# A spectral mixer on one core: sixteen f32 transforms become triples of F32R products with split constants, and the last one moves to the head of its row

## Chip, core and metric

The kernel runs on one core of a Trainium2 chip. Five engines matter: TensorE (PE in the profile, with its weight loads listed apart as PEld), VectorE (DVE), ScalarE (ACT), GpSimd (POOL) and SyncE (SP), which only starts transfers. The metric is device time in microseconds (us), the median of repeated runs. The views of the profile show one profiled execution, with its own time.

## What is computed

```python
x = A_x                                    # (1, 2048, 512)
xn = _layernorm(x)
X = rfft2(xn) * (w_r + 1j * w_i)
s = irfft2(X)                              # spectral branch
h = _layernorm(xn)                         # token-mixing branch
u = gelu(einsum("bsd,sf->bdf", h, w1) + b1)        # f = 1792
y = einsum("bdf,fs->bds", u, w2) + b2
out = x + s * silu(y.transpose(0, 2, 1))
```

Both branches start from the normalised rows of x. All inputs and outputs are float32.

## The kernel before

The 2048 tokens are laid out as 128 partitions by NJ = 16 rows; row j is a tile of 128 x 512. F32R is a 32-bit type that TensorE multiplies in one pass, with fewer bits than f32. A product that is to keep f32's accuracy is therefore made of three: with a = ah + al and b = bh + bl, where the high part is a rounding to F32R and the low part is what the rounding left, it is ah·bh + ah·bl + al·bh. The profile prints TensorE's operands as f32 for either type; on ACT and DVE the outputs of a split are printed fp32r.

**First stage (lines 388 to 521).** A loop over the rows j does three things on TensorE:

- `hidden_early(j, 4, 0, w[0], ...)`: w1's columns for four blocks of 128 hidden units times h(j), into PSUM banks 0 to 3. Four products with w1's high part and h's high part `hh[j]`, four with w1's low part and `hh[j]`, four with w1's high part and h's low part `hl[j]`. All are 128x128 weights against 512 moving columns, in F32R, on line 395.
- between the second and the third four, `first_transform(h, c)` (line 223): four f32 products that turn h(j)'s 512 channels by the constant `c`, into bank 7. The weights are h's blocks of 128 columns and the 128 columns of `c` are moving. `c` is the transform matrix `cf` times a number per token, `m["q"]`, which takes back the second normalisation; `turned` (line 217) makes it by one ACT instruction per row.
- `hidden_early(j, 3, 4, w[1], ...)`: nine more F32R products, for banks 4 to 6.

While TensorE works on row j, the other engines prepare row j + 1: ACT normalises it to `h` (line 209), rounds it to `hh` and w1's two pieces to `w1h` (line 387); DVE subtracts for the low parts `hl` and `w1l` (line 390). ACT copies bank 7 to `zt` (line 231, `first_copy`). `fold` (lines 234 to 250) combines zt's quarters into `ey`, the input of the second stage: DVE makes `o`, `e` and `t` (lines 236 to 240), POOL adds and subtracts e's halves (lines 242 and 243), ACT moves half of `o` across partitions once `t` is done (line 244), and DVE writes the last two groups of `ey` (line 247). The fold of row j is issued during row j + 1, piece by piece, because `fold` is a generator.

What fixes the order: instructions wrapped in `keep` stay on their engine in the order in which they are written; others are placed by a scheduler before the program runs. Pools hand out buffers: a tile with `bufs=1` is rewritten only after every reader of its former content is done.

**From the first stage to the second.** Row 14's turn issues three transfers `w1s` on POOL's queue (`w1_raw`, line 447), the raw w1 of the first three parts of the second batch of hidden units. After the loop `gelu(2, 2)` and `gelu(1, 1)` empty banks 2 and 1 on ACT (line 290) into `u`, `w1_high` rounds `w1s` to `w1h` on ACT, `w1_low` makes `w1l` on DVE, and `run(folds)` finishes row 15's fold.

**Second stage (lines 525 to 751).** The order of everything is written out in the string `STEPS`, one letter per piece of a stream. TensorE takes the products of the second batch (lines 678, 679, 681 and 687) in turn with the spectral filter: `along_channels` (line 586, f32, reads `ey` and `cd`, writes banks 4 to 7 in the order 7, 6, 5, 4), `forward` (line 600) and `way_back` (line 665). Before a bank can be written, the gelu that empties it must be done: bank 6, 5 and 4 by `gelu(9, 6)`, `gelu(8, 5)` and `gelu(7, 4)`.

**Third stage.** The products with w2 (line 941, F32R, 256 moving columns, three for each pair) and the inverse transforms.

Of the kernel before, what the change touches and what calls it, by code (L numbers as in the profile page):

```python
# [8 lines left out]
F32 = mybir.dt.float32  # L9
F32R = mybir.dt.float32r  # L10
BF16 = mybir.dt.bfloat16
AF = mybir.ActivationFunctionType
ALU = mybir.AluOpType
PSUM = bass.MemoryType.PSUM

P = 128
S, D, F = 2048, 512, 1792
NJ = 16
# [100 lines left out]
def spectral_mixer_kernel(tc, x, w1, b1, w2, b2, wk, we, wx, c_f, c_ft, c_d, c_i, c_g, c_h, c_s, out):  # L119
    nc = tc.nc  # L120
    V, A, G, T, SY = nc.vector, nc.scalar, nc.gpsimd, nc.tensor, nc.sync
    keep = tc.keep_in_program_order
# [8 lines left out]
    def pool(stack, side, name, bufs):  # L131
        return stack.enter_context(tc.tile_pool(name=name, bufs=bufs, side=side, reuse_waits="tile"))
# [9 lines left out]
    with tc.tile_pool(name="ps", bufs=1, space=PSUM) as psp, ExitStack() as left, ExitStack() as right:  # L142
        ps = psp.tile([P, 8, 512], F32, name="ps")
        pers = pool(left, "left", "pers", 1)
        cf = pers.tile([P, P], F32, name="cf")
# [20 lines left out]
        lnp = pool(rstage, "right", "ln", 2)  # L166
        wbp = pool(rstage, "right", "w1b", 3)
        hs = [new_hu(f"h{j}") for j in range(NJ)]
        hh, hl = [h[:, 0] for h in hs], [h[:, 1] for h in hs]
# [6 lines left out]
        def moments(nm, n):  # L176

            return {k: lnp.tile([P, 2, w], F32, name=f"{k}{nm}", tag="m" + k, bufs=3)[:, :n]  # L180
                    for k, w in (("st", 6), ("mv", 2), ("v2", 2), ("sd", 2), ("r0", 2), ("t", 2), ("rs", 2), ("nb", 1),
                                 ("q", 1))}
# [31 lines left out]
        def new_h(j):  # L214
            return lnp.tile([P, D], F32, name=f"h{j}", tag="h")

        def turned(j, m, i):

            c = lnp.tile([P, P], F32, name=f"cf{j}", tag="cfj")
            keep(A.activation(c, cf, AF.Copy, scale=m["q"][:, i]))  # L220
            return c

        def first_transform(h, c):
            z = ps[:, 7].rearrange("p (b c) -> p b c", c=P)
            for b in range(4):
                T.matmul(z[:, b], h[:, b * P:(b + 1) * P], c, start=True, stop=True)  # L226
            return z

        def first_copy(j, z):
# [37 lines left out]
        def run(steps):  # L267
            for _ in steps:
                pass
# [11 lines left out]
        def ordered(instruction):  # L281
            return keep(instruction) if strict else instruction
# [3 lines left out]
        def gelu(ft, bank):  # L286
            i, half = ft % NH, ft // NH
            if i not in raw:
                raw[i] = usp.tile([P, 2, D], F32, name=f"u{i}", tag="u")
            ordered(A.activation(raw[i][:, half], ps[:, bank], AF.Gelu_apprx_tanh, bias=b1t[:, ft:ft + 1]))  # L290
# [101 lines left out]
        def hidden_early(j, nf, bank, w, between):  # L392
            def products(wi, hj, first, last):
                for i in range(nf):
                    T.matmul(ps[:, bank + i], w[wi][:, i * P:(i + 1) * P], hj, start=first and j == 0, stop=last and j == NJ - 1)  # L395
            products(0, hh[j], True, False)
            products(1, hh[j], False, False)
            r = between()
            products(0, hl[j], False, True)
            return r  # L400

        m = moments("m0", 2)
        for i, c_ in enumerate(halves):
# [2 lines left out]
        m = {k: t[:, :1] for k, t in m.items()}  # L406
        roots(m)
        w = w1_tiles(0, *WA), w1_tiles(0, *WB)
        h = new_h(0)
# [9 lines left out]
        c = turned(0, m, 0)  # L419
# [4 lines left out]
        m = moments("m2", 2)  # L424
# [3 lines left out]
        raws_, parts, mids = {}, {}, []  # L428
# [14 lines left out]
        def w1_raw(i):  # L443
            place_, bufs = (mids[0], 1) if i % 4 == 3 else (w1p, 3)
            raws_[i] = place_.tile([P, 4 * P], F32, name=f"w1s{i}", tag="w1r", bufs=bufs)[:, :part_width(i)]
            for to, cols in w1_runs(i, raws_[i]):
                (SY if mids else G).dma_start(to, cols)

        def w1_high(i):
            parts[i] = [w1p.tile([P, 4 * P], F32R, name=f"w1{c}_{i}", tag="w1" + c)[:, :part_width(i)] for c in "hl"]  # L450
            A.activation(parts[i][0], raws_[i], AF.Copy)

        def w1_low(i):
            V.tensor_sub(parts[i][1], raws_[i], parts[i][0].bitcast(F32))
# [1 line left out]
        folds = iter(())  # L456
        for j in range(NJ):
            more = j + 1 < NJ
            if more:
                raws[j + 1, 0], raws[j + 1, 1] = w1_load(j + 1, *WA), w1_load(j + 1, *WB)  # L460
            if j == 0:
                load_x(3)
                load_x(4)
                SY.dma_start(b1t, b1)
                SY.dma_start(b2t, b2)
            if j == 4:
                SY.dma_start(cd, c_d)
                G.dma_start(cft, c_ft)
            if j in (6, 8, 10, 12):
                q = slice(16 * (j - 6), 16 * (j - 4))  # L470
                SY.dma_start(out[q, :NJ - 1], x[q, :NJ - 1])
            z = hidden_early(j, 4, 0, w[0], lambda: first_transform(h, c))
            hidden_early(j, 3, 4, w[1], lambda: None)

            early = j > 0
            if more:
                w = w1_tiles(j + 1, *WA), w1_tiles(j + 1, *WB)
                h = new_h(j + 1)
                normed(h, xs[j + 1], *of[j + 1])
                high(hh[j + 1], h)  # L480
                if early and j + 3 < NJ:
                    stats(of[j + 3][0], of[j + 3][1], xs[j + 3])
                    if j % 2 == 0:
                        spreads(of[j + 2][0], 2)
            for _ in range(3):
                next(folds, None)
            if more:
                high(w[0][0], raws[j + 1, 0])
            next(folds, None)
            if more:  # L490
                if early and j % 2 == 0 and j + 2 < NJ:
                    scales(of[j + 2][0])
                low(w[0][1], raws[j + 1, 0], w[0][0])
                if not early:
                    stats(m, 0, xs[2])
                high(w[1][0], raws[j + 1, 1])
                low(hl[j + 1], h, hh[j + 1])
                c = turned(j + 1, *of[j + 1])
                if not early:
                    stats(m, 1, xs[3])  # L500
                    spreads(m, 2)
            run(folds)
            if more:
                low(w[1][1], raws[j + 1, 1], w[1][0])
                if not early:
                    scales(m)
                if j % 2 == 0 and j + 4 < NJ:
                    m = moments(f"m{j + 4}", 2)
                    of.update({j + 4: (m, 0), j + 5: (m, 1)})
            if j + 5 < NJ:  # L510
                load_x(j + 5)
            folds = fold(j, first_copy(j, z))
            if j == NJ - 2:
                for i in range(3):
                    w1_raw(i)
        gelu(2, 2)
        w1_high(0)
        w1_low(0)
        gelu(1, 1)
        run(folds)  # L520
        w1_high(1)
        rstage.close()

# [2 lines left out]
        V, A, G, SY = map(in_order, free)  # L526
# [227 lines left out]
        V, A, G, SY = free  # L754
# [165 lines left out]
        for p in range(NP):  # L920
# [7 lines left out]
            for k, n in enumerate(ORDER):  # L928
                wf = ready.pop(0)
                w = next(wforms, None) if len(ready) < 2 else None  # L930
# [85 lines left out]
```

## Time and profile before

| what | value |
|---|---|
| median of 3 runs | 381.93 us (381.85 to 384.48) |
| the profiled execution | 382.29 us, span 380.5 us |
| TensorE busy over the span | 369.8 us, 97% |
| VectorE, ScalarE, GpSimd busy | 81%, 56%, 27% |
| granted TensorE clock | 1.00 |
| first stage, from its first product to the second stage's first | 6.33 to 98.13 us |

A span is what lies between the first and the last instruction of the program; the profiled execution's time is 1.8 us longer. "Busy" for TensorE counts a product until its modelled end, and neighbours overlap, so the spacing of starts says more about TensorE's rate than the duration of one product. A row of a timeline gives the start, the length, the engine, the line, the operation, output and inputs, the shape, the number of instructions merged into it, and in brackets the idle time before it with what ended that.

### The profile page before, as it was taken

The numbers are of one execution on the slowest core, as the hardware profiler recorded it, in microseconds if no ns is written. First come the engines' busy times: TensorE is split into PE (matmuls) and PEld (weight loads), VectorE is DVE, ScalarE is ACT, GpSimd is POOL, SyncE is SP. The second block draws the span as 40 slices with busy tenths as digits, with TensorE's granted clock in tenths as the row PEclk, the third lists the DMA queues.
The fourth block names the chain that finished last, engine by engine and source line by source line (L and its number), as shares of the span: only waits on it lengthen the run. The fifth ranks groups of instructions, "written<-read, shape, count | busy, mean of one in ns | idle before, by whom it ended". The sixth has DMA issues, their size and how long they took to land.

```text
span 380.5 us, 7482 instructions
## 1 busy us (share of the span) xinstructions
PE 369.8 (97%) x2760; PEld 327.8 (86%) x2760; DVE 309.0 (81%) x660; ACT 213.3 (56%) x384; POOL 102.3 (27%) x133
## 2 busy tenths in 40 slices
PE   8999999999999999999999799999999999999994
PEld 4888888888877676777779799999999999999994
DVE  5899999865799999999967798776767768777763
ACT  4677755754972365865456765545555555545541
POOL 2133233243511735765400011020303020200100
PEclk9999999999999999999999999999999999999999
DMA  7956467214455767999866599898888888895602
GB/s 249 323 190 231 133 222 239 91 42 128 120 196 179 253 213 258 283 280 307 194 181 155 149 267 188 265 164 263 168 246 184 223 204 193 194 217 158 100 0 56
DMA packets 41945, 73.32 MB, mean 193 GB/s; under 512 B 4180, under 2 KB 25172, under 8 KB 41780
## 3 DMA queue, kind: packets, MB, share of 16 engines
q1 hardware_dynamic: 35460, 58.88, 48.6%
q0 software_dynamic: 6448, 13.96, 21.4%
q8 instruction: 21, 0.34, 0.4%
q14 instruction: 16, 0.13, 0.1%
HBM read 60.24 MB, written 8.13 MB: 180 GB/s over the span
## 4 chain that ended last, share of the span: by engine, by line
PE 86%; DVE 8%; issue 2%; ACT 2%; DMA 1%; SPq 0%; DVEq 0%; ACTq 0%
PE ps L941 34%; PE ps L395 19%; PE ps L678 6%; PE ps L679 5%; PE ps L226 4%; PE ps L687 4%; PE ps L866 4%; PE ps L586 4%; PE ps L875 4%; DVE pq L128 2%; DVE e L128 2%; PE ps L665 1%; PE ps L681 1%; PE ps L600 1%; DMA x<-in_x_dram 1%
## 5 line engine op out<-in xcount | busy, mean ns | idle before, releaser
L395 PE MATMUL ps<-h,w1h 128*128 128x512 f32 x224 | 58.5, 398 | 0.0
L395 PEld LDWEIGHTS ps<-h,w1h 128*128 128x128 f32 x224 | 40.8, 188 | 8.1 <-ACT w1h L387 0.2
L776 DVE TENSOR_TENSOR w2f<-s,w2f 128x896 fp32r<-128x896 f32 x32 | 35.0, 1092 | 14.8 <-ACT w2f L775 13.7
L766 POOL DMA_DIRECT2D s<-in_w_dram x16 | 13.8, 865 | 122.7 <-DMA s<-in_w_dram 35.0
L678 PE MATMUL ps<-h,w1h 128*128 128x512 f32 x112 | 44.9, 401 | 0.0
L679 PE MATMUL ps<-h,w1h 128*128 128x512 f32 x112 | 43.7, 390 | 0.0
L941 PE MATMUL ps<-fb,w2f 128*128 128x256 f32 x336 | 42.9, 282 | 0.6 <-DVE c L904 0.6
L941 PE MATMUL ps<-fa,w2f 128*128 128x256 f32 x336 | 43.4, 283 | 0.0
L941 PE MATMUL ps<-fc,w2f 128*128 128x256 f32 x336 | 41.1, 279 | 2.1 <-ACT p L896 2.1
L941 PEld LDWEIGHTS ps<-fc,w2f 128*128 128x128 f32 x336 | 40.1, 188 | 2.3 <-ACT p L896 2.3
L941 PEld LDWEIGHTS ps<-fb,w2f 128*128 128x128 f32 x336 | 40.6, 188 | 1.4 <-issue 0.8
L941 PEld LDWEIGHTS ps<-fa,w2f 128*128 128x128 f32 x336 | 40.6, 188 | 0.0
L775 ACT ACTIVATE w2f<-s 128x896 fp32r<-128x896 f32 x32 | 30.3, 948 | 16.5 <-DVE s L799 13.5
L776 DVE TENSOR_TENSOR w2f<-a,w2f 128x896 fp32r<-128x896 f32 x24 | 26.1, 1089 | 15.8 <-ACT w2f L775 15.7
L128 POOL TENSOR_TENSOR s<-z,e 128x4 f32<-128x4 f32 x8 | 25.3, 3163 | 37.4 <-DMA z<-e 16.6
L775 ACT ACTIVATE w2f<-a 128x896 fp32r<-128x896 f32 x24 | 22.8, 950 | 21.7 <-PE ps L941 18.2
L395 PE MATMUL ps<-h,w1l 128*128 128x512 f32 x112 | 30.7, 390 | 0.1
L128 ACT ACTIVATE w1h<-w1s 128x512 fp32r<-128x512 f32 (+1 forms) x30 | 17.4, 581 | 22.2 <-PE ps L679 12.9
L678 PEld LDWEIGHTS ps<-h,w1h 128*128 128x128 f32 x112 | 21.0, 188 | 9.0 <-issue 5.0
L687 PE MATMUL ps<-h,w1l 128*128 128x512 f32 x93 | 25.6, 391 | 0.1
L395 PEld LDWEIGHTS ps<-h,w1l 128*128 128x128 f32 x112 | 20.9, 188 | 5.0 <-DVE w1l L390 0.5
L679 PEld LDWEIGHTS ps<-h,w1h 128*128 128x128 f32 x112 | 21.1, 188 | 4.0
(132 smaller groups left out, 730.8 us busy)
## 6 DMA issues: line engine op xcount, KB each, us to landing
a<-in_w_dram SPq DMA_DIRECT2D x24, 448.0 KB
s<-in_w_dram POOLq DMA_DIRECT2D x17, 448.0 KB, 7.0
s<-in_w_dram SPq DMA_DIRECT2D x15, 448.0 KB
w1r<-in_w_dram SPq DMA_DIRECT2D x16, 256.0 KB
z<-e SPq DMA_DIRECT2D x16, 256.0 KB
w1s<-in_w_dram SPq DMA_DIRECT2D x16, 256.0 KB
yj<-ey SPq DMA_DIRECT2D x16, 256.0 KB
x<-in_x_dram SPq DMA_DIRECT2D x15, 256.0 KB
```

The source lines that it names most:

```text
L128: return lambda *a, **k: keep(getattr(engine, name)(*a, **k))
L226: T.matmul(z[:, b], h[:, b * P:(b + 1) * P], c, start=True, stop=True)
L395: T.matmul(ps[:, bank + i], w[wi][:, i * P:(i + 1) * P], hj, start=first and j == 0, stop=last and j == NJ - 1)
L586: keep(T.matmul(pd[:, b * P:(b + 1) * P], ey[:, lo, b].rearrange("p h j -> p (h j)"), cd[:, b], start=True, stop=True))
L678: keep(T.matmul(o, wh[:, sl], hh[j], start=first, stop=False))
L679: keep(T.matmul(o, wh[:, sl], hl[j], start=False, stop=False))
L687: keep(T.matmul(ps[:, bank], wl[:, k * P:k * P + P], hh[j], start=False, stop=final))
L775: ordered(A.activation(wf[:, 0], v, AF.Copy))
L776: ordered(V.tensor_sub(wf[:, 1], v, wf[:, 0].bitcast(F32)))
L866: in_turn(j, T.matmul(pf[:, b], yj[:, b * P:(b + 1) * P], cft, start=True, stop=True))
L875: in_turn(j, T.matmul(pe[:, b % 2, b // 2], yt[:, b], ci[:, b], start=True, stop=True))
L941: in_turn(j0, T.matmul(o, wf[:, wi, i], ui, start=m + a == 0 and n in (1, 2, 5), stop=m == NH - 1 and a == 2, skip_group_check=n in (6, 3, ...
```

## The change

For rows 0 to 15 alike:

- `turned` makes three tiles instead of one: `c` (the scaled transform, f32) on POOL, its rounding `ch` to F32R on ACT, and the rest `cl = c - ch` on POOL. All three have one buffer, so row j + 1's `ch` is written after row j's transform has read it.
- `first_transform` makes twelve F32R products of 128 moving columns instead of four f32 ones: for each block of 128 channels `hh`·`ch`, `hh`·`cl` and `hl`·`ch`.
- In rows 0 to 14 the transform comes after all twelve products for banks 0 to 3, not after eight of them. In row 15 it comes ahead of them.
- Row 15's fold is finished ahead of `gelu(2, 2)`, and `w1_high` and the first `w1s` transfers are kept in the order of the program.

The diff:

```diff
         def turned(j, m, i):
-            c = lnp.tile([P, P], F32, name=f"cf{j}", tag="cfj")
-            keep(A.activation(c, cf, AF.Copy, scale=m["q"][:, i]))
-            return c
-
-        def first_transform(h, c):
+            c = lnp.tile([P, P], F32, name=f"cf{j}", tag="cfj", bufs=1)
+            ch, cl = (lnp.tile([P, P], F32R, name=f"cf{n}{j}", tag="cf" + n, bufs=1) for n in "hl")
+            keep(G.tensor_scalar(c, cf, m["q"][:, i], None, op0=ALU.mult))
+            keep(A.activation(ch, c, AF.Copy))
+            keep(G.tensor_sub(cl, c, ch.bitcast(F32)))
+            return ch, cl
+
+        def first_transform(j, c):
             z = ps[:, 7].rearrange("p (b c) -> p b c", c=P)
             for b in range(4):
-                T.matmul(z[:, b], h[:, b * P:(b + 1) * P], c, start=True, stop=True)
+                cols = slice(b * P, (b + 1) * P)
+                T.matmul(z[:, b], hh[j][:, cols], c[0], start=True, stop=False)
+                T.matmul(z[:, b], hh[j][:, cols], c[1], start=False, stop=False)
+                T.matmul(z[:, b], hl[j][:, cols], c[0], start=False, stop=True)
             return z
...
             products(0, hh[j], True, False)
             products(1, hh[j], False, False)
-            r = between()
             products(0, hl[j], False, True)
-            return r
+            return between()
...
             for to, cols in w1_runs(i, raws_[i]):
-                (SY if mids else G).dma_start(to, cols)
+                SY.dma_start(to, cols) if mids else keep(G.dma_start(to, cols))
 
         def w1_high(i):
             parts[i] = [w1p.tile([P, 4 * P], F32R, name=f"w1{c}_{i}", tag="w1" + c)[:, :part_width(i)] for c in "hl"]
-            A.activation(parts[i][0], raws_[i], AF.Copy)
+            keep(A.activation(parts[i][0], raws_[i], AF.Copy))
...
-            z = hidden_early(j, 4, 0, w[0], lambda: first_transform(h, c))
+            if j + 1 < NJ:
+                z = hidden_early(j, 4, 0, w[0], lambda: first_transform(j, c))
+            else:
+                z = first_transform(j, c)
+                hidden_early(j, 4, 0, w[0], lambda: None)
             hidden_early(j, 3, 4, w[1], lambda: None)
...
+        run(folds)
         gelu(2, 2)
         w1_high(0)
         w1_low(0)
         gelu(1, 1)
-        run(folds)
         w1_high(1)
         rstage.close()
```

How the instructions stand on TensorE in row 3, before (`cf` is row 3's scaled transform, the second `w1h`/`w1l` pair is that of banks 4 to 6; x4 means four in sequence):

```order
L395 MATMUL ps<-h_90,w1h_3_364 128x512 x4
L395 MATMUL ps<-h_90,w1l_3_365 128x512 x4
L226 MATMUL ps<-cf_395,h_368 128x128 x4
L395 MATMUL ps<-h_90,w1h_3_364 128x512 x4
L395 MATMUL ps<-h_90,w1h_3_366 128x512 x3
L395 MATMUL ps<-h_90,w1l_3_367 128x512 x3
L395 MATMUL ps<-h_90,w1h_3_366 128x512 x3
```

and now, up to the first of the four blocks (`cfh` and `cfl` are `ch` and `cl`; `h_90` holds both `hh` and `hl`):

```order
L401 MATMUL ps<-h_90,w1h_3_400 128x512 x4
L401 MATMUL ps<-h_90,w1l_3_401 128x512 x4
L401 MATMUL ps<-h_90,w1h_3_400 128x512 x4
L230 MATMUL ps<-cfh_432,h_90 128x128
L231 MATMUL ps<-cfl_433,h_90 128x128
L232 MATMUL ps<-cfh_432,h_90 128x128
```

The last three rows come three times more before the nine products of banks 4 to 6: twelve products stand where four stood, four places later in the row.

The end of the first stage on ACT, before (`zt_1226` and `zt_1274` are the copies of rows 14 and 15, `o_1263` and `o_1285` their folds' moves; `u` is a gelu's output):

```order
L231 ACTIVATE zt_1226<-ps 128x512
L451 ACTIVATE w1h_1278<-w1s_1228 128x384
L451 ACTIVATE w1h_1296<-w1s_1231 128x384
L244 ACTIVATE o_1263<-o_1263 64x128
L128 ACTIVATE w1h_1341<-w1s_1234 128x384
L231 ACTIVATE zt_1274<-ps 128x512
L290 ACT_TABLE_LOAD
L290 ACTIVATE u_1276<-ps,b1t 128x512
L290 ACTIVATE u_1282<-ps,b1t 128x512
L244 ACTIVATE o_1285<-o_1285 64x128
L128 ACTIVATE w1h_1344<-w1s_1304 128x384
L128 ACTIVATE u_1276<-ps,b1t 128x512
```

and now:

```order
L237 ACTIVATE zt_1410<-ps 128x512
L250 ACTIVATE o_1455<-o_1455 64x128
L237 ACTIVATE zt_1466<-ps 128x512
L250 ACTIVATE o_1469<-o_1469 64x128
L296 ACT_TABLE_LOAD
L296 ACTIVATE u_1480<-ps,b1t 128x512
L456 ACTIVATE w1h_1482<-w1s_1412 128x384
L296 ACTIVATE u_1486<-ps,b1t 128x512
L456 ACTIVATE w1h_1488<-w1s_1415 128x384
L128 ACTIVATE w1h_1533<-w1s_1418 128x384
L128 ACTIVATE w1h_1536<-w1s_1496 128x384
L128 ACTIVATE u_1480<-ps,b1t 128x512
```

Three roundings of `w1s` that stood ahead of row 15's `zt` now stand behind the table load, two of them between and behind the two gelus, and row 15's `o` stands ahead of the table load. The last row of either is `gelu(9, 6)`, which empties bank 6.

POOL at the same place, now (`cf_1398` and `cfl_1400` are row 15's `c` and `cl`):

```order
L221 TENSOR_SCALAR cf_1398<-cf,qm_1116 128x128
L248 TENSOR_TENSOR ey<-e_1387 128x16x8
L249 TENSOR_TENSOR ey<-e_1387 128x16x8
L452 DMA w1s_1412<-in_w_dram 128x128
L452 DMA w1s_1412<-in_w_dram 128x256
L452 DMA w1s_1415<-in_w_dram 128x128
L452 DMA w1s_1415<-in_w_dram 128x256
L452 DMA w1s_1418<-in_w_dram 128x128
L452 DMA w1s_1418<-in_w_dram 128x256
L223 TENSOR_TENSOR cfl_1400<-cf_1398,cfh_1399 128x128
```

All six transfers stand together, ahead of row 15's `cl`.

## The prediction

> **What bounds the kernel now.** I read the page's shares first, then the waits of TensorE, then one row of the first stage.
>
> ```profile
> span 380.5 us, 7482 instructions
> PE 369.8 (97%) x2760; PEld 327.8 (86%) x2760; DVE 309.0 (81%) x660; ACT 213.3 (56%) x384; POOL 102.3 (27%) x133
> PE ps L941 <- ACT p L896: 2.1, 1, 2.1
> PE ps L384 <- POOL wz L372: 1.3, 1, 1.3
> PE ps L665 <- DVE pq L128: 1.2, 2, 0.7
> PE ps L586 <- DVE ey L247: 0.4, 1, 0.4
> ```
>
> TensorE is busy from end to end, and the waits with an owner add up to about 6 us. So time that is added to TensorE's stream is added to the end. Does that hold in the first stage, where the change is? Three rows in its middle:
>
> ```profile
> 43.07:48.76 5.69, 5.69 (x30) 4.84 (x29) 5.48 (x16) 3.77 (x8) 2.56 (x5) 1.00 0.39 122
> 48.76:54.45 5.69, 5.69 (x31) 4.84 (x29) 5.44 (x20) 3.57 (x8) 1.42 (x3) 1.00 0.43 143
> 42.17 1.07 PE L395 MATMUL ps<-h,w1l 128*128 128x512 f32 x4
> 43.08 1.05 PE L226 MATMUL ps<-cf,h 128*128 128x128 f32 x8
> 43.88 1.87 PE L395 MATMUL ps<-h,w1h 128*128 128x512 f32 x7
> 48.76 1.05 PE L226 MATMUL ps<-cf,h 128*128 128x128 f32 x8
> L226 PE MATMUL ps<-cf,h 128*128 128x128 f32 x128 | 16.9, 275 | 0.0
> ```
>
> In the stretches of 5.69 us the columns are PE, PEld, DVE, ACT, POOL: TensorE is never idle, DVE is next at 5.5 (96%). In the rows below them the starts give TensorE's rate: four F32R products from 42.17 to 43.08 are 0.227 us each. A row takes 48.76 - 43.08 = 5.68; less 21 x 0.227 = 4.77 leaves 0.91 for the transform. The profile counts 128 records for 64 f32 products: each is made of two passes with a weight load of its own. Eight passes in 0.91 are 0.113 each, and from the first start to the last end (1.05 less one duration of 0.275, over seven) 0.111. I take 0.112 us a pass, 0.90 a row.
>
> **What the twelve products cost.** No row shows an F32R product with 128 moving columns, so I bound it. Below, by streaming: 0.227 us for 512 columns, and for 256
>
> ```profile
> 299.76 3.46 PE L941 MATMUL ps<-fc,w2f 128*128 128x256 f32 x28
> ```
>
> (3.46 - 0.28) / 27 = 0.118. The slope, 0.109 for 256 columns, gives 0.063 us for 128. But each product also needs its 128x128 weights loaded, and one load is visible by itself, where TensorE stood waiting for `w1l` in row 0:
>
> ```profile
> 7.64 0.19 PEld L395 LDWEIGHTS ps<-h,w1l 128*128 128x128 f32 x1 [0.49 <-DVE w1l L390]
> 7.64 0.30 PEld L395 LDWEIGHTS ps<-h,w1l 128*128 128x128 f32 x2 [0.49 <-DVE w1l L390]
> L395 PE MATMUL ps<-h,w1l x112: 387/389/504, 7.6 to 97.2; 128*128 128x512 f32 x112
> 1.33 0.13 PEld L384 LDWEIGHTS <-wz 128*128 128x128 bf16 x2 [1.33 <-POOL wz L372]
> ```
>
> The first F32R load after the wait takes 0.19 us and the second starts 0.30 - 0.19 = 0.11 later, with nothing ahead of it but the first; the product that needed the first load took 504 ns, 115 more than the median 389. Two bf16 loads fit into 0.13. So an F32R load occupies the loader for 0.11 us. Behind a product of 0.227 or 0.118 that is hidden; behind one of 0.063 it isn't. I therefore price each of the twelve at 0.112, as much as an f32 pass: 12 x 0.112 = 1.34 a row against 0.90, so +0.448, and over 16 rows **+7.2 us**. Ends of the range: 0.109 (12 x 0.109 - 0.90 = 0.41, 6.6 us) and 0.118, the spacing of the 256-column products if the load, not the stream, sets it (0.52, 8.3 us).
>
> Could two products that share their weights share a load? `hh`·`ch` and `hh`·`cl` follow each other with the same weights. So do lines 678 and 679 now:
>
> ```profile
> L678 PEld LDWEIGHTS ps<-h,w1h 128*128 128x128 f32 x112 | 21.0, 188 | 9.0 <-issue 5.0
> L679 PEld LDWEIGHTS ps<-h,w1h 128*128 128x128 f32 x112 | 21.1, 188 | 4.0
> ```
>
> 112 loads for 112 products on each: no load is saved.
>
> [...]
>
> **The side chain of `ch` and `cl`.** Each row gains two POOL instructions of 128x128 and keeps one on ACT. Nearest rows:
>
> ```profile
> L242 POOL TENSOR_TENSOR ey<-e 128x128 f32<-128x128 f32 x16 | 9.1, 570 | 49.2 <-DVE e L237 49.2
> L220 ACT ACTIVATE cf<-cf,qm 128x128 f32<-128x128 f32 x16 | 6.2, 387 | 0.0
> L447 POOL DMA_DIRECT2D w1s<-in_w_dram x6 | 3.3, 551 | 1.0 <-DVE w1l L390 1.0
> 87.47 1.09 POOL L447 DMA_DIRECT2D w1s<-in_w_dram x2 [0.99 <-DVE w1l L390]
> ```
>
> With one buffer, `ch` of row j + 1 waits for transform j; behind it on ACT stand `o` and `zt`, behind it on POOL `cl`. The chain is 0.2 (TensorE's end to ACT's start) + 0.39 + 0.57 = 1.2 us, while the next transform starts 9 + 12 products later, 4.8 us. For row 15, whose transform comes first, only nine products later, 2.0 us, with the three pairs of `w1s` transfers ahead of `cl` on POOL. They take 3.3 us; the last pair waits for row 15's `w1l` and starts at 87.47 now, 5 us ahead of row 15 (21 products and a transform ahead of 98.13, at 92.46), so it and `cl` fit. Hidden; uncovered, it would cost TensorE what it is late.
>
> POOL slows DVE where they meet:
>
> ```profile
> 48.01 0.51 POOL L243 TENSOR_TENSOR ey<-e 128x128 f32<-128x128 f32 x1
> 43.94 0.69 DVE L390 TENSOR_TENSOR w1l<-w1r,w1h 128x512 fp32r<-128x512 f32 x1
> 48.23 0.84 DVE L390 TENSOR_TENSOR w1l<-w1r,w1h 128x512 fp32r<-128x512 f32 x1
> ```
>
> The same subtraction takes 0.84 us beside POOL's, 0.69 without: 0.15 for each POOL instruction, 0.3 a row. DVE's 5.5 us become 5.8, in a row that is now 5.68 + 0.45 = 6.13. Still under it: no cost, and later rows, with less on DVE, have more room.
>
> **The head of the stage.** Row 1's transform waits today for bank 7, since ACT copied row 0's `zt` late.
>
> ```profile
> 15.21 1.16 PE L226 MATMUL ps<-cf,h 128*128 128x128 f32 x8
> ```
>
> It should start at 14.40 + 3 x 0.227 = 15.08 and takes 1.16 instead of 1.05: 0.2 us lost. Now it comes later than that copy: **-0.2**.
>
> **The seam between the stages.** Now:
>
> ```profile
> 89.66 0.60 ACT L231 ACTIVATE zt<-ps 128x512 f32<-128x512 f32 x1 [2.17 <-PE ps L226]
> 90.15 0.93 ACT L451 ACTIVATE w1h<-w1s 128x384 fp32r<-128x384 f32 x2
> 91.87 0.31 ACT L244 ACTIVATE o<-o 64x128 f32<-64x128 f32 x1 [0.79 <-DVE t L240]
> 95.34 0.60 ACT L231 ACTIVATE zt<-ps 128x512 f32<-128x512 f32 x1 [2.61 <-PE ps L226]
> 95.96 1.28 ACT L290 ACT_TABLE_LOAD   x1
> 97.25 1.27 ACT L290 ACTIVATE u<-ps,b1t 128x512 f32<-128x512 f32 x2
> 98.88 0.52 ACT L128 ACTIVATE w1h<-w1s 128x384 fp32r<-128x384 f32 x1
> 99.31 1.25 ACT L128 ACTIVATE u<-ps,b1t 128x512 f32<-128x512 f32 x2
> 94.25 1.05 PE L226 MATMUL ps<-cf,h 128*128 128x128 f32 x8
> 98.13 0.40 PE L678 MATMUL ps<-h,w1h 128*128 128x512 f32 x1
> 98.60 0.60 PE L586 MATMUL ps<-cd,ey 128*128 128x128 f32 x4
> 99.57 3.42 PE L586 MATMUL ps<-cd,ey 128*128 128x128 f32 x28 [0.37 <-DVE ey L247]
> ```
>
> Four passes at 98.60 end by 99.05; the next begin at 99.57 and, after a load of 0.11, run at 99.68: 0.63 us lost to row 15's late fold. With the transform ahead, that fold is done while TensorE is still on row 15, and this stall goes. What is late next is ACT. Counting from the start of row 15 (0): the transform ends at 1.34, `zt` starts at 1.53, `o` 2.21 later (as 91.87 - 89.66) at 3.74, ends at 4.05; the table load ends at 5.36; the first gelu starts there, the first `w1h` 0.59 later at 5.95, ending at 6.47. TensorE is through row 15 at 6.11 and needs this `w1h`: with the load it runs at 6.64, 0.53 lost. In the old order it was made at 90.15, long before. Two products and eight passes bring TensorE to 7.99, where it needs bank 6, so `gelu(9, 6)`. ACT's starts go on: second gelu 6.38, three `w1h` at 6.97, 7.39 and 7.81 (0.42 apart, as 0.93 for two), `gelu(9, 6)` at 8.24, ending at 8.92 and letting TensorE run at 9.04: 1.05 lost. After that banks 5 and 4 are free in time. So 1.58 in place of 0.63: **+1.0**, between -0.6 (all of it hidden) and +1.6 (nothing of the old stall back).
>
> **Sum.** 7.2 - 0.2 + 1.0 = **+8.0 us**: the profiled execution from 382.29 to 390.3, its span from 380.5 to 388.5. That execution is 0.36 above the median of the runs shown, so the median goes from 381.93 to **389.9**. The ends of the bounds: 6.6 - 0.2 - 0.6 = 5.8 and 8.3 + 1.6 = 9.9, so 387.7 to 391.8.
>
> **Rivals.**
>
> Loads that don't show (chance 0.07). In a stream the loader may run ahead of narrow products as it can't after a stall; from 0.90 / 12 = 0.075 us a product downward the change gains. At the streamed 0.063 it gives -2.2 - 0.2 + 1.0, or 380.5; with the seam at its best 378.9. For: 0.063 is what the slope says. Against: two loads at the stall 0.11 apart. This is the case that is not slower.
>
> A spacing half way between stream and load (0.05), 0.0875: 12 x 0.0875 - 0.90 = 0.15 a row, 2.4 in all, plus 0.8 for the seam and the head: 385.1. [...]
>
> Narrow F32R products fall back to f32's two passes (0.05). No row shows F32R under 256 columns. 24 passes x 0.112 = 2.69, +1.79 a row, 28.7 in all: 411.
>
> DVE takes over (0.09). If the two POOL instructions cost DVE one for one, 2 x 0.57 = 1.1, its 5.5 become 6.6 against 6.13: +0.5 in the ten or so rows that are full, 5 us more: 395. For: DVE at 96%. Against: 0.15, not 0.57, in the row above.
>
> **Chances and range.** The forecast keeps 0.74. A measurement tells about 1% (3.8 us) from no change: slower by over 1%, above 385.7, are the forecast, the two passes and DVE, 0.88; within 1% the spacing half way and most of the first rival, 0.10; faster by over 1% what a better seam than mine would add to that, 0.02. The range, 387.0 to 395.0, holds the forecast's bounds and DVE's case.
>
> **What would show it.** Right: the transform's twelve products start 0.11 us apart and a row takes 6.1 us, with TensorE still without a gap; each has its own load; line 586's wait for `ey` is gone, and TensorE waits at the seam for ACT, once for the first `w1h` and once for a gelu. Wrong: starts 0.06 apart (then the loader was the error), waits of the transform for POOL's `cl`, or DVE without idle time and TensorE waiting for `w1l`.

## The result and the profile after

| | before | after |
|---|---|---|
| median of 6 runs each, on the same chip | 382.09 us (381.85 to 384.48) | 391.48 us (391.18 to 392.29) |
| ratio, 95% interval | | 1.0227 [1.0201, 1.0252] |
| the profiled execution, its span | 382.29, 380.5 us | 391.77, 390.0 us |
| TensorE busy | 369.8 us | 377.6 us |

The change costs 9.4 us; 8.0 were forecast (389.9 us, range 387.0 to 395.0). In some executions of most versions here the mean granted clock is 0.995 and not 1.00 and the time about 2 us longer, which the last section takes up, and one execution of the order without the triples (410.22 us at a clock of 0.851) is left out of its figures.

TensorE is still the bound. From the page of the kernel after:

```profile
span 390.0 us, 7658 instructions
PE 377.6 (97%) x2824; PEld 335.3 (86%) x2824; DVE 312.1 (80%) x660; ACT 213.4 (55%) x384; POOL 122.5 (31%) x165
```

Two rows of the first stage, by the same columns as before (PE, PEld, DVE, ACT, POOL, granted clock, DMA share, GB/s), and one row's transform on TensorE:

```profile
43.00:49.13 6.13, 6.13 (x34) 5.28 (x33) 5.55 (x19) 3.24 (x7) 2.82 (x6) 1.00 0.81 291
49.13:55.26 6.13, 6.13 (x34) 5.28 (x33) 4.49 (x10) 3.94 (x9) 3.08 (x6) 1.00 0.37 120
```

```profile
47.11 0.22 PE L230 MATMUL ps<-cfh,h 128*128 128x128 f32 x1
47.17 0.27 PE L231 MATMUL ps<-cfl,h 128*128 128x128 f32 x1
47.28 0.28 PE L232 MATMUL ps<-cfh,h 128*128 128x128 f32 x1
47.40 0.28 PE L230 MATMUL ps<-cfh,h 128*128 128x128 f32 x1
...
48.29 0.27 PE L232 MATMUL ps<-cfh,h 128*128 128x128 f32 x1
...
53.24 0.22 PE L230 MATMUL ps<-cfh,h 128*128 128x128 f32 x1
```

Read the starts, not the durations. 53.24 - 47.11 = 6.13 us a row, where it was 5.68. Within a transform the starts stand 0.11 apart, whether the weights are new (L232 to L230) or the same as the product's before (L230 and L231 both use `hh`); only the first step is 0.06. The rows of PEld say why: the loads start at 46.89, 47.11, 47.22 and 47.33. The first product's weights were loaded 0.22 us ahead of it, under the product before; each later product starts 0.06 behind the start of its own load, and the loads stand 0.11 apart. There are as many loads as products, 64 on each of the three lines:

```profile
L232 PEld LDWEIGHTS ps<-cfh,h 128*128 128x128 f32 x64 | 12.3, 192 | 0.0
L231 PEld LDWEIGHTS ps<-cfl,h 128*128 128x128 f32 x64 | 12.2, 191 | 0.6
```

TensorE's waits after the change (total, times, longest), without those that are in both kernels alike:

```profile
PE ps L950 <- DVE c L913: 1.4, 2, 0.8
...
PE ps L595 <- ACT u L128: 0.8, 1, 0.8
PE ps L687 <- ACT w1h L456: 0.7, 1, 0.7
```

The wait for `ey` is gone and the two for ACT have come, as forecast. On TensorE and on ACT the seam now reads:

```profile
104.98 0.84 PE L401 MATMUL ps<-h,w1h 128*128 128x512 f32 x3
106.49 0.50 PE L687 MATMUL ps<-h,w1h 128*128 128x512 f32 x1 [0.67 <-ACT w1h L456]
106.83 0.40 PE L688 MATMUL ps<-h,w1h 128*128 128x512 f32 x1
107.07 1.05 PE L595 MATMUL ps<-cd,ey 128*128 128x128 f32 x8
108.89 1.49 PE L595 MATMUL ps<-cd,ey 128*128 128x128 f32 x11 [0.76 <-ACT u L128]
```

```profile
101.10 0.31 ACT L250 ACTIVATE o<-o 64x128 f32<-64x128 f32 x1 [2.16 <-DVE t L246]
101.44 0.60 ACT L237 ACTIVATE zt<-ps 128x512 f32<-128x512 f32 x1
103.72 0.31 ACT L250 ACTIVATE o<-o 64x128 f32<-64x128 f32 x1 [1.68 <-DVE t L246]
104.04 1.28 ACT L296 ACT_TABLE_LOAD   x1
...
105.92 0.51 ACT L456 ACTIVATE w1h<-w1s 128x384 fp32r<-128x384 f32 x1
```

Three products from 104.98 end their stream at 105.66. The first product of the second stage gets its `w1h` at 106.43, issues at 106.49 and runs at about 106.60 after its load: 0.94 us lost. Eight passes from 107.07 end by 107.96; the next run at 109.00: 1.04 lost. On ACT row 15's `zt` follows row 14's `o` (101.10), and the table load stands behind row 15's `o` and ahead of all that TensorE waits for.

**Where the 9.5 us of the span went.** Rows 16 x 0.44 = 7.1. Row 1's stall gone, -0.2. Seam (0.94 + 1.04) - 0.63 = +1.35. These are 8.3. Two pieces lie outside the forecast: the head of the program, +0.7, and one wait for `c` in the third stage (L950 <- DVE c L913, one more than before), +0.8; that is 0.3 more than there is to share out, which is the rounding of sixteen rows and the ends of waits. The head, of before and then of after:

```profile
1.34 5.32 PE L384 MATMUL ps<-wz 128*128 128x512 bf16 x16 [1.34 <-POOL wz L372]
6.33 1.25 PE L395 MATMUL ps<-h,w1h 128*128 128x512 f32 x4
```

```profile
1.34 6.41 PE L390 MATMUL ps<-wz 128*128 128x512 bf16 x16 [1.34 <-POOL wz L378]
7.40 1.28 PE L401 MATMUL ps<-h,w1h 128*128 128x512 f32 x4
```

The same sixteen warm-up products take 1.09 us longer. Each takes 0.427 us until the clock rises and 0.216 from there; it rose at 4.8 us in the one execution and at 7.0 in the other. (Before lost 0.3 to 0.4 of it again to a wait for `w1l`.)

### The profile page after: what moved, and what is told of

The parts are those of the page before. It is cut to its first block, busy times and chain, and to the rows that moved or that the text cites. A ratio compares the mean times of both kernels' runs of the same rounds, so it can differ in the third digit from the quotient of the medians.

```text
span 390.0 us, 7658 instructions
## 1 busy us (share of the span) xinstructions
PE 377.6 (97%) x2824; PEld 335.3 (86%) x2824; DVE 312.1 (80%) x660; ACT 213.4 (55%) x384; POOL 122.5 (31%) x165
## 4 chain that ended last, share of the span: by engine, by line
PE 84%; DVE 10%; ACT 2%; issue 2%; POOL 0%; DVEq 0%; ACTq 0%; POOLq 0%
PE ps L950 31%; PE ps L401 18%; PE ps L687 5%; PE ps L688 5%; PE ps L696 4%; PE ps L595 4%; PE ps L884 3%; PE ps L875 3%; DVE pq L128 2%; PE ps L232 2%; PE ps L231 2%; PE ps L390 2%; DVE e L128 2%; PE ps L230 2%; PE ps L674 1%
## 5 line engine op out<-in xcount | busy, mean ns | idle before, releaser
L401 PE MATMUL ps<-h,w1h 128*128 128x512 f32 x224 | 60.0, 395 | 0.0
L401 PEld LDWEIGHTS ps<-h,w1h 128*128 128x128 f32 x224 | 40.9, 188 | 7.7
L687 PE MATMUL ps<-h,w1h 128*128 128x512 f32 x112 | 45.0, 402 | 0.7 <-ACT w1h L456 0.7
L950 PE MATMUL ps<-fb,w2f 128*128 128x256 f32 x336 | 42.7, 281 | 1.4 <-DVE c L913 1.4
L688 PE MATMUL ps<-h,w1h 128*128 128x512 f32 x112 | 43.7, 391 | 0.0
L950 PE MATMUL ps<-fa,w2f 128*128 128x256 f32 x336 | 43.4, 283 | 0.0
L950 PE MATMUL ps<-fc,w2f 128*128 128x256 f32 x336 | 41.0, 279 | 2.1 <-ACT p L905 2.1
L950 PEld LDWEIGHTS ps<-fb,w2f 128*128 128x128 f32 x336 | 40.5, 188 | 2.3 <-ACT w2f L784 1.0
L950 PEld LDWEIGHTS ps<-fc,w2f 128*128 128x128 f32 x336 | 40.1, 188 | 2.3 <-ACT p L905 2.3
L950 PEld LDWEIGHTS ps<-fa,w2f 128*128 128x128 f32 x336 | 40.7, 188 | 0.0
L687 PEld LDWEIGHTS ps<-h,w1h 128*128 128x128 f32 x112 | 21.0, 188 | 10.0 <-issue 5.0
L919 POOL DMA_DIRECT2D out_dram<-g x15 | 15.0, 1000 | 31.3 <-DVE g L917 31.3
```

What stands on the lines that cost most here:

```text
L687: keep(T.matmul(o, wh[:, sl], hh[j], start=first, stop=False))
L688: keep(T.matmul(o, wh[:, sl], hl[j], start=False, stop=False))
L919: G.dma_start(out[:, j, cols], g[:, cols], accum_op=ALU.add)
L950: in_turn(j0, T.matmul(o, wf[:, wi, i], ui, start=m + a == 0 and n in (1, 2, 5), stop=m == NH - 1 and a == 2, skip_group_check=n in (6, 3, ...
```

## The experiments

All ratios are to the kernel before, measured on the same chip along with the variant. For the first four experiments five of its seven runs had a clock of 0.995 or 0.996 (384.1 to 384.5 us, beside 381.9 and 382.6), so these four ratios come out lower than the kernel before at a clock of 1.00 would give; compare the times and spans. The order of the instructions in the second and third stage is that of the kernel after in all of them, unless the edit says otherwise.

### Columns or loads: two of three products on 64 columns

```diff
-                T.matmul(z[:, b], hh[j][:, cols], c[1], start=False, stop=False)
-                T.matmul(z[:, b], hl[j][:, cols], c[0], start=False, stop=True)
+                T.matmul(z[:, b, :64], hh[j][:, cols], c[1][:, :64], start=False, stop=False)
+                T.matmul(z[:, b, :64], hl[j][:, cols], c[0][:, :64], start=False, stop=True)
```

> The changed kernel, with the second and third product of each block on only 64 of the 128 moving columns (so half of the correction terms is left out). Twelve loads as before, two thirds of the columns (4 x (128 + 64 + 64) = 1024 in place of 1536). If the loads set the pace (my theory): starts stay 0.11 us apart, a transform stays at 1.34 us, a row at 6.13, the span at 390. [...]

Measured: 390.97 us (2 runs), ratio 1.0191 [1.0134, 1.0248], rows of 6.11 us. From TensorE's timeline:

```profile
47.32 0.30 PE L230 MATMUL ps<-cfh,h 128*128 128x128 f32 x1
47.46 0.25 PE L231 MATMUL ps<-cfl,h 128*128 128x64 f32 x1
47.55 0.28 PE L232 MATMUL ps<-cfh,h 128*128 128x64 f32 x1
47.66 0.31 PE L230 MATMUL ps<-cfh,h 128*128 128x128 f32 x1
```

A third of the columns is gone (4 x 128 of 12 x 128), and a block still takes 47.66 - 47.32 = 0.34 us, three loads of 0.11. The steps inside the block shift with the columns, 0.14, 0.09 and 0.11, their sum doesn't. Columns don't set the pace: the loads do, or something else that comes once with each product. The next two experiments tell these apart.

### The same columns with a third fewer loads

`ch` and `cl` lie side by side in one tile, so `hh` is loaded once for 256 moving columns; a block is then two products. `c[1]` is now that tile of 256 columns. The two halves of the wide result aren't added, and the blocks overwrite each other.

```diff
-                T.matmul(z[:, b], hh[j][:, cols], c[0], start=True, stop=False)
-                T.matmul(z[:, b], hh[j][:, cols], c[1], start=False, stop=False)
-                T.matmul(z[:, b], hl[j][:, cols], c[0], start=False, stop=True)
+                two = ps[:, 7, b % 2 * 256:b % 2 * 256 + 256]
+                T.matmul(two, hh[j][:, cols], c[1], start=True, stop=False, skip_group_check=True)
+                T.matmul(two[:, :P], hl[j][:, cols], c[0], start=False, stop=True, skip_group_check=True)
```

> The changed kernel, with ch and cl side by side in one tile, so that hh's weights are loaded once and meet 256 moving columns, and hl's meet 128: eight products and loads in place of twelve, the columns the same (4 x (256 + 128) = 1536). The two halves of the wide result aren't added, and blocks overwrite each other in bank 7, so the sum of the terms is left out. Loads set the pace: 4 x 0.118 + 4 x 0.112 = 0.92 us a transform, a row 5.69, 16 x 0.42 = 6.7 us less than the changed kernel: a span of 383. [...]

Measured: 388.21 us (2 runs), ratio 1.0119 [1.0066, 1.0172]. TensorE's timeline and two of its waits:

```profile
44.75 0.34 PE L232 MATMUL ps<-cfb,h 128*128 128x256 f32 x1
44.92 0.22 PE L233 MATMUL ps<-cfb,h 128*128 128x128 f32 x1
44.98 0.33 PE L232 MATMUL ps<-cfb,h 128*128 128x256 f32 x1
45.15 0.22 PE L233 MATMUL ps<-cfb,h 128*128 128x128 f32 x1
```

```profile
PE ps L232 <- POOL cfb L224: 1.3, 1, 1.3
...
PE ps L232 <- ACT zt L238: 0.4, 1, 0.4
```

A block takes 44.98 - 44.75 = 0.23 us, two loads, so the loads' theory has the transform right, though four products went with the four loads. The span, 386.4 us, missed its 383: rows were 5.78 and, every other one, 5.9 us instead of 5.69, and row 15's transform waited 1.3 us for POOL's `cl`. With TensorE's row down by 0.35, the side chain of `c`, `ch`, `cl` and `zt` shows. Both runs had a mean clock of 0.996 or less, which is about another 1.6 us (below).

### Weights that load faster

The upper sixteen bits of the same tiles, read as bf16: the same count of products, loads and columns, with fewer bits.

```diff
-                T.matmul(z[:, b], hh[j][:, cols], c[0], start=True, stop=False)
-                T.matmul(z[:, b], hh[j][:, cols], c[1], start=False, stop=False)
-                T.matmul(z[:, b], hl[j][:, cols], c[0], start=False, stop=True)
+                top = [t.bitcast(BF16)[:, 1::2] for t in (hh[j][:, cols], hl[j][:, cols], c[0], c[1])]
+                T.matmul(z[:, b], top[0], top[2], start=True, stop=False)
+                T.matmul(z[:, b], top[0], top[3], start=False, stop=False)
+                T.matmul(z[:, b], top[1], top[2], start=False, stop=True)
```

> The changed kernel, with the twelve products on the upper 16 bits of the same F32R tiles, read as bf16 (the lower bits are left out of the products; no instruction is added on the other engines). Same count, same columns, and the first loads of the kernel, which are bf16, stood within 0.13 us for two. Loads set the pace: with quick loads the starts are 0.056 to 0.065 us apart, a transform 0.7 to 0.8, 16 x 0.58 = 9 us less: a span of 381. [...] If something else holds any product of 128 columns at 0.11 (the write into the bank, the change of weights): 390, unchanged.

Measured: 387.99 us (2 runs), ratio 1.0113 [1.0059, 1.0168]. Two rows of TensorE's timeline, and its waits:

```profile
44.34 0.22 PE L232 MATMUL ps<-cfl,h 128*128 128x128 bf16 x1
44.40 0.22 PE L233 MATMUL ps<-cfh,h 128*128 128x128 bf16 x1
44.45 0.22 PE L231 MATMUL ps<-cfh,h 128*128 128x128 bf16 x1
...
50.37 0.22 PE L231 MATMUL ps<-cfh,h 128*128 128x128 bf16 x1 [0.28 <-ACT zt L238]
```

```profile
PE ps L688 <- ACT w1h L457: 1.7, 1, 1.7
...
PE ps L231 <- ACT zt L238: 1.3, 5, 0.3
```

Twelve products from 44.26 end their stream 0.69 us later, 0.058 apart; 0.058 is what 128 of 512 columns take by streaming (0.227 / 4 = 0.057). So a product of 128 columns has no floor of its own at 0.11, and the F32R load, 0.11 us, is what held it there. With bf16 loads the twelve products are cheaper than f32's eight passes (0.90). This is the rival in which loads don't show, with bf16 weights.

The span, 385.7 us, again missed its 381. Rows mostly alternate between 5.55 and 6.12 us, with a wait for ACT's `zt` in the long ones. The likely reason, not tested, is that the preparation that DVE, ACT and POOL do for two rows at once takes as long as it did, and a TensorE that is 0.6 us a row faster runs into it. The clock was 0.996 here too.

### Without POOL in the chain

ACT makes `ch` itself and `ch` stands in for `cl`, so that POOL does nothing for it.

```diff
-            c = lnp.tile([P, P], F32, name=f"cf{j}", tag="cfj", bufs=1)
-            ch, cl = (lnp.tile([P, P], F32R, name=f"cf{n}{j}", tag="cf" + n, bufs=1) for n in "hl")
-            keep(G.tensor_scalar(c, cf, m["q"][:, i], None, op0=ALU.mult))
-            keep(A.activation(ch, c, AF.Copy))
-            keep(G.tensor_sub(cl, c, ch.bitcast(F32)))
-            return ch, cl
+            ch = lnp.tile([P, P], F32R, name=f"cfh{j}", tag="cfh", bufs=1)
+            keep(A.activation(ch, cf, AF.Copy, scale=m["q"][:, i]))
+            return ch, ch
```

> The changed kernel without POOL's two instructions a row: ACT makes ch directly from the scaled constant, and ch stands in for cl (so the correction by cl is left out). TensorE's products are the same in number and size. My theory: the side chain on POOL, ACT and DVE is hidden, so nothing changes but noise: ratio to the kernel before 1.02 to 1.025, rows of 6.13 us. Rival: POOL's instructions slow DVE and hold TensorE somewhere; then the time falls by more than 1 us, and TensorE's waits on DVE or POOL in the first stage with it.

Measured: 390.58 us (4 runs), ratio 1.0184 [1.0143, 1.0226]. The ratio is a little under the 1.02 to 1.025 that was expected; it is one of the four that come out low. The same stretch as above, without POOL's two instructions a row:

```profile
43.00:49.13 6.13, 6.13 (x35) 5.29 (x34) 5.57 (x21) 3.85 (x9) 2.29 (x4) 1.00 0.43 161
```

The row is 6.13 us again and DVE's busy time the same (5.57, beside 5.55 with POOL's work). At 6.13 us the side chain is hidden. The 1.4 us of span between the two kernels are, in the main, the head (first product at 6.85, not 7.40) and the third stage's wait for `c` (0.6, not 1.4); TensorE's first wait at the seam is 0.2 shorter as well.

### The order without the triples

The kernel after with f32 transforms and ACT's `c` as before: the new place in the row, the last row's transform first, the new seam.

```diff
-            c = lnp.tile([P, P], F32, name=f"cf{j}", tag="cfj", bufs=1)
...
+            c = lnp.tile([P, P], F32, name=f"cf{j}", tag="cfj")
+            keep(A.activation(c, cf, AF.Copy, scale=m["q"][:, i]))
+            return c
...
+                T.matmul(z[:, b], h[:, b * P:(b + 1) * P], c, start=True, stop=True)
```

> The kernel before, with f32 transforms and one ACT instruction for the constants, and only the order of the change: transforms after all twelve products of banks 0 to 3, row 15's at the head of its row, the fold ahead of the gelus, the roundings of w1s kept behind them. My theory: a row keeps its 5.68 us; at the seam the wait for the fold (0.63) goes and TensorE waits for the first w1h (0.5) and for the gelu of bank 6 (1.1): +1.0; row 1's stall of 0.2 goes: 382.9 against 382.1, ratio 1.002. Rival: the seam's waits are made good later, since the other engines gain the same time: 381.9, ratio 0.9995, with the waits seen all the same.

Measured: 383.70 us (11 runs), ratio 1.0017 [0.9995, 1.0039]; rows 5.69. The ratio says "no difference", but ten of the 23 runs of the kernel before beside it had a clock of 0.994 to 0.996, and only two of these eleven. At a clock of 1.00 this kernel takes 383.7 (nine runs), the kernel before 382.0 (13) and the kernel after 391.4 (four). So the triples carry 7.7 of the 9.4 us and the order 1.7, twice the 0.8 that was expected of it. Its seam on TensorE:

```profile
97.84 0.84 PE L395 MATMUL ps<-h,w1h 128*128 128x512 f32 x3
98.97 0.50 PE L681 MATMUL ps<-h,w1h 128*128 128x512 f32 x1 [0.29 <-ACT w1h L450]
...
101.36 2.05 PE L589 MATMUL ps<-cd,ey 128*128 128x128 f32 x16 [0.77 <-ACT u L128]
```

The two waits for ACT are there without a single triple: 0.56 and 1.04 us lost by the same count as above, +1.0 against the 0.63 of before. Less row 1's 0.2, and with a head that is 0.7 longer in this execution too (first product at 7.32), that is 1.5, beside 1.4 by the two spans.

### The seam mended

In the kernel after, the first two roundings of `w1s` go back ahead of row 15's `zt` on ACT, and row 15's fold behind the gelus, as before; the transform of row 15 stays at the head of its row.

```diff
+            if not more:
+                w1_high(0)
+                w1_high(1)
             early = j > 0
...
-        run(folds)
         gelu(2, 2)
-        w1_high(0)
         w1_low(0)
         gelu(1, 1)
-        w1_high(1)
+        run(folds)
```

> The changed kernel with its seam mended: the first two roundings of w1s stand on ACT right behind row 14's zt, and the two gelus ahead of row 15's fold; row 15's transform stays at the head of its row. My theory: the first stage is as long as in the changed kernel (rows of 6.13 us), and neither wait is left at the seam (2.0 us in the changed kernel), so 389.5 against 391.5, ratio to the kernel before 1.018 (1.0227 for the changed kernel). Rival: ACT is short of time there in any order, and the waits move to another reader: the same 391.5.

Measured: 390.11 us (6 runs), ratio 1.0179 [1.0148, 1.021]. No wait is left at the seam:

```profile
104.18 0.84 PE L401 MATMUL ps<-h,w1h 128*128 128x512 f32 x3
104.86 0.39 PE L688 MATMUL ps<-h,w1h 128*128 128x512 f32 x1
...
105.32 3.73 PE L596 MATMUL ps<-cd,ey 128*128 128x128 f32 x32
```

Five of these runs had a clock of 0.995 or 0.996 (median 390.2); the one at 1.00 took 388.5, 6.5 above the 382.0 that the kernel before takes at 1.00 (13 runs). That one run is what rows, stall and seam give: 7.1 - 0.2 - 0.6 = 6.3.

### The mended order without the triples

The same edit in the kernel with f32 transforms: the order's part of the change alone, at its best. Against the kernel before, beside that edit:

```diff
-            r = between()
             products(0, hl[j], False, True)
-            return r
+            return between()
...
-            z = hidden_early(j, 4, 0, w[0], lambda: first_transform(h, c))
+            if j + 1 < NJ:
+                z = hidden_early(j, 4, 0, w[0], lambda: first_transform(h, c))
+            else:
+                z = first_transform(h, c)
+                hidden_early(j, 4, 0, w[0], lambda: None)
```

> The mended seam with f32 transforms: what of the change is left when the twelve products are taken out and the seam is put right. My theory: rows of 5.68 us, no wait at the seam (0.63 in the kernel before), row 1's stall gone (0.2): 381.2 against 382.1, ratio 0.9977, so faster than both kernels by little. Rival: the seam's time is given back to a wait in the second or third stage: ratio 1.000.

Measured: 383.19 us (12 runs), ratio 0.9992 [0.9967, 1.0017]: no difference, though the seam has no wait and the stage's rows are as before. The profile shows why. From 215 to 225 us, the kernel before and this one (columns as above):

```profile
215.00:225.00 10.00, 10.00 (x89) 10.00 (x89) 7.11 (x15) 7.69 (x12) 0.70 (x2) 1.00 0.84 225
```

```profile
215.00:225.00 10.00, 10.00 (x75) 10.00 (x74) 5.77 (x11) 7.35 (x11) 0.27 (x1) 0.83 0.88 205
```

TensorE is as busy and gets 14 products fewer done: its granted clock is 0.5 for one stretch of 3.41 us (0.83 on average here), and this costs 1.6 us at once (14 at 0.112 to 0.118). In the two of the twelve runs with a mean clock of 1.00 the kernel took 380.83 and 381.02, 1.1 below the kernel before at that clock; in the ten at 0.995 or 0.996 its median is 383.3.

### Filling the wait ahead of the slow stretch

The slow stretch in the profile above begins at 215.34 us, 1.1 us behind the end of TensorE's longest wait, 2.1 us for ACT's `p` as the third stage begins. Sixteen products into a bank that nobody reads yet fill it, once in the kernel before and once in the one above.

```diff
+                if p == 0 and k == 3:
+                    for _ in range(16):
+                        in_turn(j0, T.matmul(ps[:, 7, :HD], *spare, start=True, stop=True))
                 for m, i in enumerate(FORMS):
...
+                spare = wf[:, 0, i], uh
```

> The kernel before, with sixteen idle products (128x256 F32R, into a bank that nobody reads yet) put where TensorE waits 2.1 us for ACT's p at the change to the third stage. Theory: that wait is what sometimes makes the throttle give TensorE a granted clock of 0.5 for the next 3.41 us, and that is the 1.6 to 2 us by which some executions of the same program are longer. Sixteen products of 0.117 us fill 1.87 of the 2.11 us and delay nothing, so the mean clock is 0.999 or 1.00 in all runs, none lies near 384, and the median is 382.0 plus at most 0.2. Rival: the drop comes from something else (the head of the program, or a throttle that counts work and not waits): then mean clocks of 0.995 go on in about four runs of ten, at 384.1.

> The same sixteen products in the kernel with f32 transforms, the change's order and the mended seam, in which ten of twelve runs had a mean clock of 0.995 or 0.996 (median 383.3) and two had 1.00 (380.8 and 381.0). Theory: all runs at a clock of 0.999 or 1.00, median 380.9, 1.1 us (0.3%) under the kernel before at a clock of 1.00 and 1.2 under its median. Rival, the drop comes from elsewhere: most runs stay at 0.995 and 383.3.

Measured: in the kernel before 382.68 us (381.98 to 383.24, 12 runs), ratio 0.9992 [0.9973, 1.0011]; in the mended order 381.69 us (380.97 to 382.83, 12 runs), ratio 0.9972 [0.9952, 0.9991]. The wait as it is now, in the second of them:

```profile
211.52 2.05 PE L944 MATMUL ps<-fc,w2f 128*128 128x256 f32 x16
213.79 2.74 PE L948 MATMUL ps<-fc,w2f 128*128 128x256 f32 x21 [0.22 <-ACT p L900]
```

No run of the 24 has a clock under 0.997 and none lies above 383.3, where 9 of the 23 runs of the kernel before beside them were at 0.995 or 0.996 and 383.6 to 384.4. So the wait brings the slow stretch on. The medians missed by 0.5 and 0.8 us: runs now scatter over 1.3 to 1.9 us, some with a clock of 0.997 or 0.998, of which the profile of the second shows one thing, a lower clock in the last microseconds, 0.83 from 375 to 380 us (1.00 in the kernel before); TensorE has only 0.66 us of work there. Part of the scatter lies outside the span: the run of 382.83 us has a span of 379.9, 2.9 less, where 1.8 is usual. What else is in it stays open. The mended order with f32 transforms and the filled wait is the one version here that is faster than both kernels, by 0.3% of the kernel before; against that kernel's 14 runs at a clock of 1.00 (381.9) it is 0.2 us, under 0.1%, and that is not clear of the scatter.

## Why the prediction was right, and where not

- **TensorE is the bound**: right. 7.1 of the 9.5 us of the span came in the rows, one for one, and TensorE stayed busy for 97%.
- **Twelve products at a load each, +0.448 a row**: right. 6.13 against the forecast 6.13; starts 0.11 apart where 0.06 had been the rival. Three things show that the load is the reason: a third of the columns taken away changes nothing; a third of the loads taken away, with their products, takes the transform back to 0.92; and with bf16 weights the same twelve products follow each other at 0.058. The last one rules out that the product itself takes 0.11.
- **Products with the same weights share no load**: right, 64 loads for 64 products on each line.
- **The side chain is hidden, DVE 5.8 us**: hidden at 6.13, and DVE stayed at 5.55; over the whole program its busy time grew by 3.1 us, 0.2 a row and not 0.3. The sum for POOL was wrong in a part that cost nothing: the scaled constant on POOL takes 1.04 us on average, not the 0.57 of a subtraction. The two faster transforms show how little cover there was: at rows of 5.7 or 5.5 it is most likely the side chain that sets every other row.
- **Row 1's stall, -0.2**: right; that row is 6.13 like the others.
- **Seam, +1.0**: the mechanism right, both waits in the places named, the size short by 0.4: 1.35. The gelu cost 1.04 of the forecast 1.05; the first `w1h` cost 0.94, not 0.53. The step that failed is "`zt` starts at 1.53": row 15 begins at 105.66 - 6.11 = 99.55, so that would be 101.08, but row 14's `o` held ACT until 101.41 and `zt` started at 101.44, 0.36 late. From there the chain kept the forecast's distances (`o` 2.28 and not 2.21 behind `zt`), and `w1h` ended 0.77 us behind TensorE's row, not 0.36. The forecast had moved the transform forward in the row, but not looked at what ACT does at that moment. The gelu cost no more than forecast since TensorE came to it as much later as ACT did.
- **Missed altogether**: +0.7 at the head and +0.8 in the third stage. The head is the moment at which the clock rises during the warm-up products. The first real product follows that moment in different kernels: 6.33 us for a rise at 4.80 (before), 6.34 for 4.88 (the 256-column products), 7.40 for 7.01 (after) and 7.45 for 7.13 (the mended order with f32 transforms). Triples and the new order stand at both ends, so neither fixes it: it is when the clock rose in the profiled execution (last section), and as far as these profiles show, this part of the difference between the two spans is luck. The third stage's second wait for `c` (0.80 us at 299) is in the profiles of after and of the one with 64 columns (0.46), and in none of the other kernels with the same order: it isn't tied to the change by any run.
- By run times, after (391.4, four runs at a clock of 1.00) is 9.4 above before (382.0), and the forecast was 8.0: the rows and the side chain came as reasoned, and what the sum lacks is, in the main, 0.4 at the seam and the two pieces just named, which the width of the range took in. The mended seam took 2.9 of the 9.4 back in its one run at that clock, of which the seam itself explains 2.0. The rest is of the size of the two pieces just named.

**The rivals.** Loads that don't show, and a spacing half way: not in F32R (0.11 us), the first in bf16 (0.058, beside the rival's 0.063). Two passes: no, one record and one load for each product. DVE as the bound: no, not at 6.13; but TensorE waited for ACT's `zt` or POOL's `cl` as soon as it was quicker.

## What to carry to other kernels

Count loads before columns: in a train of products here each cost the larger of its stream and its weight load. With F32R weights of 128x128 a load took 0.11 us, so 64, 128 and 256 columns cost about the same (a block of three took 0.34 us with 128 columns each and 0.34 with 128, 64 and 64; 256 columns took 0.118 in a train), and three F32R products of 128 columns (0.335 us) are half as dear again as one f32 product of two passes (0.225). Where one operand is split, put its two parts side by side as moving columns behind one load: a block took 0.23 us so, not 0.34. A step that is moved past another engine's queue (here ACT's table load, 1.28 us) is paid for at the place where that queue is next needed, and when a stage is made shorter, look at what was hidden under the old length before counting the gain.

## What was not expected of the hardware

A single wait of TensorE of 2.1 us, in a stream that is otherwise full, can halve its granted clock for 3.41 us and cost 1.6 us more than itself. By their mean clock of 0.994 to 0.996 (3.41 us at a half of 382 is 0.0045) it did so in 5 of 7, 10 of 23 and 9 of 23 executions of the kernel before, in 10 of 12 of the mended order, and in none of 24 once the wait was filled with idle products. In the profile of the mended order the stretch is 3.413 us long. The wait of 2.1 us is in nine of the eleven profiles here; their mean clock is 0.995 or 0.996 in four and 0.999 or 1.00 in five.

Why only in some executions? The clock records of three traces suggest it. After its first rise the clock changes only after whole multiples of 3.4133 us: after 110 of them in the kernel before (375.466 us), after 112 in the kernel after (382.293 us), and after 61, 1 and 48 in the mended order with f32 transforms (208.213, 3.413 and 163.840 us). So in these three it looks decided window by window. Where the windows lie differs between executions: the first rise comes at 4.80 us in the kernel before, at 7.01 in the kernel after and at 7.13 in the mended order, though the warm-up products start at 1.34 in the first two alike. The windows around the wait, in the mended order and then in the kernel before (columns: PE busy, granted clock, DMA share, GB/s):

```profile
211.93:215.34 3.41, 1.30 (x11) 1.00 0.04 13
215.34:218.75 3.41, 3.41 (x18) 0.50 0.89 168
```

```profile
209.60:213.01 3.41, 2.68 (x23) 1.00 0.75 233
213.01:216.42 3.41, 2.03 (x17) 1.00 0.17 21
```

In the first the whole wait, 2.11 us, lies in one window, and the next window is the slow stretch. In the second an edge cuts the wait into 0.73 and 1.38 us, and the clock stays at 1.00. In the kernel after the edge at 222.05 us cuts it into 0.94 and 1.17 us, and the clock stays at 1.00 too. By these three profiles the limit lies between 1.38 and 2.11 us of idle time in a window; where, no run here shows, and no kernel here has a profile of both kinds. The slowed runs of the kernel before are 2.1 to 2.2 us longer than its others, about 0.5 more than the stretch costs; a later rise of the clock at the head, which hangs on the same windows, would account for that, but it is not shown.
